# One more wo chunk kept on chip, a 2 KB zero source, and zero writes at other places in a two-layer decode backward

## The chip, the cores and the metric

The kernel runs on one core of one Trainium2 chip. The metric is the device time of the execution in microseconds; the median of five runs is 452.57 us. Engines are named as in the profile: PE (matrix), PEld (its weight loads), DVE (vector), ACT (scalar), POOL (GpSimd) and SP (which here only issues DMAs).

## What is computed

The forward pass of four residual steps on one token of width 1024 (attention, MLP, attention, MLP, with the same weights both times), and its gradients. The output is the token after the four steps, and the gradients of the token, both caches and all weights.

```python
def _A_ref(x, k_cache, v_cache, wq, wo):      # 32 query heads of 128, 4 cache heads
    W = min(4096, max(256, Sk // 4))          # Sk = 32768: the last 4096 rows count
    k, v = k_cache[:, :, Sk - W:, :], v_cache[:, :, Sk - W:, :]   # each repeated for 8 heads
    p = softmax(einsum("bhqd,bhkd->bhqk", (x @ wq) heads, k) * Dh ** -0.5)
    return einsum("bhqk,bhkd->bhqd", p, v) flat @ wo              # wo: 4096 x 1024
def _B_ref(x, w1, b1, w2):                    # F = 3584
    h = x @ w1 + b1
    return (h * tanh(softplus(h))) @ w2
x = x + _A_ref(layernorm(x), ...)   # A1
x = x + _B_ref(layernorm(x), ...)   # B2
x = x + _A_ref(layernorm(x), ...)   # A3
x = x + _B_ref(layernorm(x), ...)   # B4
# reference: x, and vjp of x with respect to A_x, both caches, wq, wo, w1, b1, w2
```

Two consequences matter here. The gradient of each cache is zero outside the last 4096 rows, yet the whole output has to be written: 2 x 4 heads x 28672 rows x 128 in bf16 are 58.7 MB of zeros. And each weight is needed more than once, while the on-chip memory can't hold all of them.

## The kernel before

**Stages.** The order is A1 forward, B2 forward (with the backward products of w2 that B4's gradient needs), A3 forward, "the turn" B4 (`mlp_turn`: forward and backward through w1 block by block), A3 backward, the second pass over w2 (`W2Pass.rest`, which finishes B4's output and gives B2's gradient), B2's w1 pass (`mlp_bwd_w1`), A1 backward, and a last part (L1207 on) that forms all weight and cache gradients as outer products and writes them. Engines run a hand-written order: each issues its instructions in the program's order and waits on what it needs.

**Data on chip.** K, V and wq stay on chip. wo has 16 chunks of 256 rows (512 KB each); chunks 0 to NR - 1 stay in `wo_b`, with NR = 9. The other chunks of wo ("late"), w1 and w2 are streamed through the pool `strm`, which has NB = 6 slots of 4 KB per partition. A load into a slot can be issued when the last reader of the slot is done; SP issues all loads in program order, so a load that waits for a slot holds up whatever stands behind it.

**wo's late chunks.** There are 7 of them for 6 slots in A3 forward (L465 to L467 and L555), A3 backward and A1 backward (L798, and `T` at L807). So six are asked for ahead, and the seventh when a slot comes free. In `attn_fwd` the first 13 (second layer) chunks go through wide matmuls into one row bank and the last 3 through small ones (`fwd_rows2`); `order` (L541) takes one late chunk, then the kept ones, then the other late ones. In `attn_bwd` each late chunk costs one block of eight PE transposes with an ACT copy, and one DVE multiply-and-sum at L813; kept chunks 0 to 7 go through 32 wide matmuls (L833), and the kept chunk 8 through `bwd_rows2` (16 small ones), from weights that `fill` transposed before, in B4. After its loads, A1 backward calls `zeros(Z["A1d"])` (L860).

**Zeros.** 112 jobs of 512 KB each write from one on-chip tile of zeros `zt`, 128 partitions of 4 KB. `bg_zeros(n, after)` (L133) issues n of them on POOL, behind a one-column copy (`gate_t`) that waits until `after` is written; `zeros(n)` (L127) issues n on SP. The table `Z` (L1133) says how many at each place: 76 on POOL in all, in the order B2 (at the w2 loop's last chunk but one), A3 (after q), the seven blocks of B4, A3 backward at its beginning (A3c) and after its loads (A3d), the w1 pass, A1 backward (A1c); the remaining 36 on SP (A1d), ahead of all gradient writes in SP's order.

**Work in gaps.** `fill` takes transposes of wo, V, K and wq (for later stages) from queues, in the order given; `warm(n)` issues n matmuls of 512 columns that nothing reads. Three hooks put w2 work of the second pass into gaps of A3 backward: `copy` (transposes of chunk 0), `sel` (the rest of chunk 0) and `ln` (chunks 1 and 2).

**Constants.** `onesD` is a 128 x 128 fp32 tile of 1/1024, the weights of the matmuls that sum over partitions in the layer norms. `pat` is four copies of a 128 x 32 pattern `fold`; its one 128-column matmul sums each head's column over four groups (L529, L913). `pad_cols` keeps four copies of a 32-column result for `row_layout` to transpose at once.

Of the kernel before, what the change touches and what calls it, by code (L numbers as in the profile page):

```python
# [8 lines left out]
FP32 = mybir.dt.float32  # L9
# [10 lines left out]
NR = 9  # L20
# [3 lines left out]
def kernel(  # L24
# [74 lines left out]
    onesD = keep.tile([P, P], FP32, name="onesD")  # L99
    nc.vector.memset(onesD[:], invD)  # L100
# [15 lines left out]
    zt = keep.tile([P, ZC], BF16, name="zt")  # L116
    nc.gpsimd.memset(zt[:], 0.0)

    zero_jobs = []
    per = ZR // P * DH  # L120
    for out_t in (out_2, out_3):
        for g in range(G):
            zflat = out_t[0, g, 0:ZR, :].rearrange("(p r) d -> p (r d)", p=P)
            for i in range(per // ZC):
                zero_jobs.append(zflat[:, i * ZC:(i + 1) * ZC])

    def zeros(n):  # L127
        for _ in range(min(n, len(zero_jobs))):
            nc.sync.dma_start(zero_jobs.pop(0), zt[:])
# [3 lines left out]
    def bg_zeros(n, after):  # L133
# [3 lines left out]
        for _ in range(min(n, len(zero_jobs))):  # L137
            nc.gpsimd.dma_start(zero_jobs.pop(0), zt[:])  # L138
# [123 lines left out]

    pre = []
# [13 lines left out]
    def ln_fwd(x_col, name):  # L277
# [4 lines left out]
        nc.tensor.matmul(sps[:], lhsT=onesD[:], rhs=xx[:], start=True, stop=True)  # L282
# [17 lines left out]
    def ln_bwd(dn_ps, n32, rstd, g_col, name, nxt):  # L300
# [5 lines left out]
        nc.tensor.matmul(sps[:], lhsT=onesD[:], rhs=tt[:], start=True, stop=True)  # L306
# [83 lines left out]
    def row_layout(col32, name):  # L390
        x = area[name].rearrange("p (g d) -> p g d", g=G)
        ps = psum1([P, P], BF16, "rps")
        nc.tensor.transpose(ps[:, 0:P], col32[:], ident_bf[:])
# [8 lines left out]
    def pad_cols(pad, src_ps, sc, name):  # L402
        nc.scalar.activation(pad[:].rearrange("p (g x) -> p g x", x=40)[:, :, 0:8],
                             src_ps.rearrange("p (g h) -> p g h", g=G), ACT.Copy, scale=sc)
        rep = keep.tile([P, NC, HQ], BF16, name=name + "_rep")
        nc.vector.tensor_copy(
            rep[:].rearrange("p c (g h) -> p c g h", g=G),
            pad[:].rearrange("p (g x) -> p g x", x=40)[:, None, :, 0:8].to_broadcast([P, NC, G, 8]))
# [24 lines left out]
    def attn_fwd(x_col, lname, first):  # L433
# [73 lines left out]
        nc.vector.tensor_scalar(out=sdg[:, 0:32], in0=pat[:, 0, :], scalar1=ssum[:, 0:1], scalar2=None, op0=ALU.mult)  # L507
        sps = sm_tile(P, HQ)
        nc.tensor.matmul(sps[:, 0:32], lhsT=onesD[:], rhs=sdg[:, 0:32], start=True, stop=True)
# [19 lines left out]
        nc.tensor.matmul(lps[:], lhsT=pat[:].rearrange("p c x -> p (c x)"), rhs=ssum[:], start=True, stop=True)  # L529
# [11 lines left out]
        order = early + late if first else late[0:1] + early + late[1:]  # L541
        for i, c in enumerate(order):
# [12 lines left out]
            if not first and i == 0:  # L555
                held[NO - 1] = wo_load(NO - 1)
# [49 lines left out]
    class W2Pass:  # L606
# [33 lines left out]
        def rest(self, done, g_bf, x_col, xname, gbc, zn, last=None):  # L640
            for c in range(NW2):
# [9 lines left out]
                if c == NW2 - 2 and zn:  # L651
                    bg_zeros(zn, self.wg[:, c, :])
# [8 lines left out]
    def mlp_fwd(x_col, lname, g_bf):  # L661
# [5 lines left out]
        gbc = bcast_row(g_bf)  # L667
        for i in range(2 * TD):
            t, hf = i // 2, i % 2
            w = w1_load(i)  # L670
            for b in range(NW2):
# [121 lines left out]
    def attn_bwd(g_col, g_bf, lname, sv, first, nxt):  # L793
# [36 lines left out]
        bwd_rows2(dacc, wo_kept[NR - 1], NR - 1, g_bf, started=False)  # L830
# [7 lines left out]
        if not first:  # L838
# [7 lines left out]
                lambda: row_layout(sA3["dorep"][:].rearrange("p c x -> p (c x)"), "do3"),  # L846
                lambda: row_layout(sA3["qrep"][:].rearrange("p c x -> p (c x)"), "q3"),
# [44 lines left out]
        else:  # L892
# [6 lines left out]
                lambda: row_layout(sA1["dorep"][:].rearrange("p c x -> p (c x)"), "do1"),  # L899
                lambda: row_layout(sA1["qrep"][:].rearrange("p c x -> p (c x)"), "q1"),  # L900
# [11 lines left out]
        for hf in range(2):  # L912
            nc.tensor.matmul(lps[:], lhsT=pat[:].rearrange("p c x -> p (c x)"), rhs=sdp[:, hf:hf + 1], start=hf == 0, stop=hf == 1)  # L913
# [43 lines left out]
    def col_out(cols, n, out_flat):  # L957
        ps = psum1([2 * HQ, P], BF16, "rw")
        nc.tensor.transpose(ps[0:n, 0:P], cols, ident_bf[:])
        rt = work.tile([2 * HQ, P], BF16, name="rt", tag="rt")  # L960
# [172 lines left out]
    Z = dict(B2=3, A3=16, B4=[5, 2, 1, 2, 1, 2, 6], A3c=6, A3d=26, W1=3, A1c=3, A1d=36)  # L1133
# [4 lines left out]
    pat = keep.tile([P, NC, 32], FP32, name="pat")  # L1138
# [6 lines left out]
    fold16f = work.tile([HQ, NO], FP32, name="fold16f")  # L1145

    def constants():
        nc.vector.reduce_sum(fold[:], ident_f[:].rearrange("p (c x) -> p x c", c=NC), axis=AX.X)
        nc.vector.tensor_copy(pat[:], fold[:, None, :].to_broadcast([P, NC, 32]))
# [106 lines left out]
```

## Time and profile before

| | |
|---|---|
| median of 5 runs (451 to 457) | 452.57 us |
| the profiled execution, its own time | 454.31 us |
| its span, first to last instruction | 452.2 us |
| PE, DVE, ACT, POOL busy | 325.1, 236.6, 225.1, 56.8 us |
| DMA | 172.25 MB, mean 381 GB/s |
| queue of SP (q1), of POOL (q0) | 131.61 MB, 39.86 MB |
| zeros | 76 on POOL, 36 on SP, 512 KB each |
| loads of late wo chunks | 28, of 512 KB |

The profiler recorded one execution. "Busy" is time in which an engine had an instruction in work, as a part of the whole span; the stages have different limits, so the shares say little about any one of them. The page's second part cuts the span into 40 equal slices of 11.3 us; a digit is a busy share in tenths, the row of GB/s is what DMA moved in the slice. The stages lie about here: A1 forward to 68 us, B2 to 111, A3 forward to 142, B4 to 188, A3 backward to 246, the second w2 pass to 266, the w1 pass to 295, A1 backward to 338, the gradients to the end. A row of the timeline has the start, the duration, engine, line, operation, output and inputs, shape and count; in brackets stands the idle time of the engine before it and what ended it. "SPq" and "POOLq" are DMAs issued there.

### The profile page before, as it was taken

What the parts mean: (1) busy time and instruction counts of PE and PEld (TensorE: products, weight loads), DVE (VectorE), ACT (ScalarE), POOL (GpSimd) and SP (SyncE); (2) the same over time, 40 slices, a digit from 0 to 9 for tenths busy, and PEclk for the clock granted to TensorE, in tenths of its full rate; (3) what the DMA queues carried; (4) which work ended last, traced back from release to release, by engine and by line L of the source; (5) the groups of instructions that cost most, each with busy time, mean ns of one, the idle gap of its engine ahead of it and who ended that gap; (6) DMA issues with size and microseconds to landing.
All of it is one profiled execution on the core that took longest, in us unless ns stands there. A gap on an engine that the chain in (4) does not pass through costs nothing.

```text
span 452.2 us, 11941 instructions
## 1 busy us (share of the span) xinstructions
PE 325.1 (72%) x5107; PEld 221.0 (49%) x5107; DVE 236.6 (52%) x489; ACT 225.1 (50%) x262; POOL 56.8 (13%) x146
## 2 busy tenths in 40 slices
PE   0565755488997989878899788777877669997400
PEld 0233524387466989855797788744631111121000
DVE  3124101188322757763265954472349889999700
ACT  1122100075242858874484554336219989989600
POOL 2000000001431211432340020042010000000000
PEclk9999555578876989995689678899885555555555
DMA  7999997999999999999998999899999999999994
GB/s 321 381 411 424 408 408 292 409 339 306 416 416 392 397 336 336 398 413 418 414 416 346 328 348 335 310 328 417 416 415 419 419 417 417 419 417 420 417 417 180
DMA packets 52257, 172.25 MB, mean 381 GB/s; under 512 B 5200, under 2 KB 12396, under 8 KB 51180
## 3 DMA queue, kind: packets, MB, share of 16 engines
q1 hardware_dynamic: 41120, 131.61, 75.1%
q0 software_dynamic: 11040, 39.86, 22.1%
q8 instruction: 40, 0.66, 0.6%
q14 instruction: 13, 0.11, 0.1%
q10 hardware_dynamic: 44, 0.01, 0.0%
HBM read 72.89 MB, written 98.58 MB: 379 GB/s over the span
## 4 chain that ended last, share of the span: by engine, by line
PE 19%; DMA 12%; ACT 12%; issue 5%; DVE 3%; POOL 1%; DVEq 0%; SPq 0%; ACTq 0%; POOLq 0%
PE tps L193 7%; ACT wq_b L148 5%; DMA w_c<-in_B_w_dram 4%; PE ops L229 4%; PE acc L229 3%; DMA out_dram<-wo_b 3%; DMA out_dram<-st_o 2%; DMA wo_c<-in_A_wo_dram 2%; ACT wo_b L148 2%; ACT st_o L148 1%; PE d L229 1%; ACT wo_c L148 1%; PE tps L623 1%; ACT K L148 1%; PE sm L229 1%
## 5 line engine op out<-in xcount | busy, mean ns | idle before, releaser
L138 POOL DMA_DIRECT2D out_dram<-zt x76 | 40.6, 537 | 45.1 <-DMA out_dram<-zt 42.5
L229 PEld LDWEIGHTS <-w_c 128*128 128x128 bf16 x1120 | 36.0, 101 | 18.4 <-DMA w_c<-in_B_w_dram 14.2
L229 PE MATMUL ops<-V 2*128 2x512 bf16 (+1 forms) x160 | 34.8, 598 | 5.9 <-ACT wq_b L148 3.3
L633 ACT COPY w_c<-tps 128x1024 bf16<-128x1024 bf16 x28 | 28.2, 1012 | 20.7 <-PE tps L623 11.4
L647 DVE CUSTOM_DVE_ANT_0 scr<-w_c,gbc 128x1024 bf16<-128x1024 bf16 x28 | 34.2, 1221 | 3.7 <-DMA w_c<-in_B_w_dram 2.1
L145 DVE CAST wq_b<-ops 128x1024 bf16<-128x1024 f32 (+1 forms) x31 | 33.8, 1149 | 3.8 <-PE ops L229 3.3
L148 ACT CAST wq_b<-ops 128x1024 bf16<-128x1024 f32 (+1 forms) x33 | 33.7, 1140 | 2.2 <-PE ops L229 2.0
L148 ACT COPY K<-tps 128x1024 bf16<-128x1024 bf16 x19 | 18.7, 1030 | 29.5 <-PE tps L193 29.5
L229 PE MATMUL ops<-wo_b 2*128 2x512 bf16 x120 | 23.3, 568 | 10.9 <-ACT wq_b L148 7.1
L229 PEld LDWEIGHTS <-V 128*128 128x128 bf16 (+2 forms) x416 | 14.1, 101 | 27.8 <-issue 27.6
L229 PE MATMUL q<-wq_b,nA_pair 128*32 128x512 bf16 x128 | 11.9, 454 | 16.3 <-DMA wq_b<-in_A_wq_dram 16.3
L623 PE MATMUL tps<-ident_bf,w_c 128*128 128x128 bf16 x224 | 22.2, 259 | 0.6 <-DMA w_c<-in_B_w_dram 0.6
L148 ACT COPY w_b<-tps 128x1024 bf16<-128x1024 bf16 x20 | 19.5, 1015 | 5.9 <-PE tps L193 5.8
L193 PE MATMUL tps<-ident_bf,w_c 128*128 128x128 bf16 x224 | 19.0, 252 | 4.6 <-DMA w_c<-in_B_w_dram 4.6
L145 DVE COPY K<-tps 128x1024 bf16<-128x1024 bf16 x13 | 8.8, 689 | 24.8 <-PE tps L193 23.0
L193 PE MATMUL tps<-ident_bf,K 128*128 128x128 bf16 x256 | 20.4, 240 | 0.2 <-ACT K L148 0.2
L148 ACT COPY w_c<-tps 128x768 bf16<-128x768 bf16 (+1 forms) x14 | 11.6, 829 | 17.5 <-PE tps L193 17.2
L813 DVE CUSTOM_DVE_ANT_0 wo_c<-wo_c,gbc 128x1024 bf16<-128x1024 bf16 x14 | 16.4, 1218 | 7.3 <-DMA wo_c<-in_A_wo_dram 5.7
L229 PEld LDWEIGHTS <-wo_b 2*128 2x128 bf16 (+1 forms) x152 | 5.6, 99 | 29.3 <-issue 28.6
L145 DVE COPY w_c<-tps 128x1024 bf16<-128x1024 bf16 (+1 forms) x18 | 11.7, 661 | 14.9 <-PE tps L193 10.2
L193 PE MATMUL tps<-ident_bf,wq_b 128*128 128x128 bf16 x256 | 18.4, 241 | 0.9 <-issue 0.9
L193 PEld LDWEIGHTS <-K 128*128 128x128 bf16 x256 | 17.1, 108 | 3.8 <-issue 3.2
(323 smaller groups left out, 664.6 us busy)
## 6 DMA issues: line engine op xcount, KB each, us to landing
out_dram<-zt POOLq DMA_DIRECT2D x76, 512.0 KB, 10.5
out_dram<-zt SPq DMA_DIRECT2D x36, 512.0 KB, 8.7
wo_c<-in_A_wo_dram SPq DMA_DIRECT2D x28, 512.0 KB, 8.4
w_c<-in_B_w_dram SPq DMA_DIRECT2D x32, 448.0 KB, 6.4
w_c<-in_B_w_dram SPq DMA_DIRECT2D x28, 512.0 KB, 6.4
out_dram<-wq_b SPq DMA_DIRECT2D x17, 512.0 KB, 11.5
wq_b<-in_A_wq_dram SPq DMA_DIRECT2D x16, 512.0 KB, 11.2
out_dram<-K SPq DMA_DIRECT2D x8, 1024.0 KB, 12.8
```

What stands on the lines that cost most here:

```text
L138: nc.gpsimd.dma_start(zero_jobs.pop(0), zt[:])
L145: nc.vector.tensor_copy(out_ap, in_ap)
L148: nc.scalar.copy(out_ap, in_ap)
L193: nc.tensor.transpose(ps[:, b, :], ap, ident_bf[:])
L229: nc.tensor.matmul(out_ap, lhsT=lhsT, rhs=rhs, start=start, stop=stop, skip_group_check=True, **kw)
L623: nc.tensor.transpose(self.ps[c][:, b, :], w[:, 1, b * P:(b + 1) * P], ident_bf[:])
L633: nc.scalar.copy(self.w[c][:, 1, :], self.ps.pop(c)[:].rearrange("p b c -> p (b c)"))
L647: nc.vector.tensor_tensor_reduce(out=scr[:], in0=w[:, 0, :], in1=gbc[:], scale=1.0, scalar=0.0, op0=ALU.mult, op1=ALU.add, accum_out=self. ...
L813: nc.vector.tensor_tensor_reduce(out=w[:, 0, :], in0=w[:, 0, :], in1=gbc[:], scale=1.0, scalar=0.0, op0=ALU.mult, op1=ALU.add, accum_out=w ...
```

## The change

- NR is 10: chunk 9 of wo stays on chip as well, and 6 late chunks are streamed, so all six are asked for ahead and the late seventh load is gone (L555 and its like). `order` in the second forward attention takes three late chunks first. `attn_bwd` runs `bwd_rows2` for chunks 8 and 9.
- The memory for it comes from smaller constants: `zt` has 2 KB per partition, and each zero job reads it twice (a broadcast dimension of 2 in the source); `onesD` is one column, read as a broadcast; `pat` is gone, and `over_groups` issues four 32-column matmuls with `fold`; `pad_cols` keeps one copy, and `row_layout` issues four 32-column matmuls into an fp32 bank; two small tiles share buffers with others.
- Zeros: two at B2's w1 loop (new, B2a), two at the first w2 chunk of B2 (new) and three at the last but one as before, 17 for 16 in A3, B4's blocks 1, 2, 2, 2, 2, 2, 3 for 5, 2, 1, 2, 1, 2, 6, A3d 24 for 26, two at chunk 2 of the second w2 pass (new), 4 for 3 at the w1 pass. That is 77 on POOL and 35 on SP.
- In B2 the row copy `gbc` is made after four chunks of w1 instead of ahead of the first.
- The hooks issue 3, 2 and 4 warm matmuls more, and `ln` takes chunk 1 alone; chunk 2 goes back to the second pass.

```diff
-NR = 9
+NR = 10
...
-    onesD = keep.tile([P, P], FP32, name="onesD")
-    nc.vector.memset(onesD[:], invD)
+    ones1 = keep.tile([P, 1], FP32, name="ones1")
+    nc.vector.memset(ones1[:], invD)
+    onesD = ones1[:, 0:1].to_broadcast([P, P])
...
-    zt = keep.tile([P, ZC], BF16, name="zt")
+    zt = keep.tile([P, ZC // 2], BF16, name="zt")
     nc.gpsimd.memset(zt[:], 0.0)
+    zt2 = zt[:, None, :].to_broadcast([P, 2, ZC // 2])
...
-                zero_jobs.append(zflat[:, i * ZC:(i + 1) * ZC])
+                zero_jobs.append(zflat[:, i * ZC:(i + 1) * ZC].rearrange("p (a b) -> p a b", a=2))
...
-            nc.sync.dma_start(zero_jobs.pop(0), zt[:])
+            nc.sync.dma_start(zero_jobs.pop(0), zt2)
...
-            nc.gpsimd.dma_start(zero_jobs.pop(0), zt[:])
+            nc.gpsimd.dma_start(zero_jobs.pop(0), zt2)
...
+    def over_groups(out, rhs, start, stop):
+        for c in range(NC):
+            mm(out[32 * c:32 * c + 32, :], fold[:], rhs, start, stop, tile_position=(0, 32 * c))
...
-        ps = psum1([P, P], BF16, "rps")
-        nc.tensor.transpose(ps[:, 0:P], col32[:], ident_bf[:])
+        ps = psum1([P, P], FP32, "rps")
+        for c in range(NC):
+            mm(ps[32 * c:32 * c + 32, 0:P], col32[:], ident_bf[:], True, True, tile_position=(0, 32 * c))
...
-        nc.tensor.matmul(lps[:], lhsT=pat[:].rearrange("p c x -> p (c x)"), rhs=ssum[:], start=True, stop=True)
+        over_groups(lps, ssum[:], True, True)
...
-        order = early + late if first else late[0:1] + early + late[1:]
+        order = early + late if first else late[0:3] + early + late[3:]
...
-            if not first and i == 0:
-                held[NO - 1] = wo_load(NO - 1)
...
-                if c == NW2 - 2 and zn:
-                    bg_zeros(zn, self.wg[:, c, :])
+                if c in zn:
+                    bg_zeros(zn[c], self.wg[:, c, :])
...
-        gbc = bcast_row(g_bf)
         for i in range(2 * TD):
             t, hf = i // 2, i % 2
             w = w1_load(i)
+            if i == 4:
+                gbc = bcast_row(g_bf)
+                bg_zeros(Z["B2a"], n_bf)
...
-        bwd_rows2(dacc, wo_kept[NR - 1], NR - 1, g_bf, started=False)
+        for c in range(8, NR):
+            bwd_rows2(dacc, wo_kept[c], c, g_bf, started=c > 8)
...
-    Z = dict(B2=3, A3=16, B4=[5, 2, 1, 2, 1, 2, 6], A3c=6, A3d=26, W1=3, A1c=3, A1d=36)
+    Z = dict(B2a=2, B2={0: 2, NW2 - 2: 3}, A3=17, B4=[1, 2, 2, 2, 2, 2, 3], A3c=6, A3d=24, B4w={2: 2}, W1=4, A1c=3, A1d=37)
...
-    hooks.update(copy=lambda: w2p.tp(0), sel=lambda: w2_ahead([0]), ln=lambda: w2_ahead([1, 2]))
+    def copy_gap():
+        w2p.tp(0)
+        warm(3)
+
+    def sel_gap():
+        w2_ahead([0])
+        warm(2)
+
+    def ln_gap():
+        w2_ahead([1])
+        warm(4)
+
+    hooks.update(copy=copy_gap, sel=sel_gap, ln=ln_gap)
     g2, g2b = attn_bwd(g3, g3b, "A3", sA3, True, "B2")
-    x4, wg2 = w2p.rest(3, g2b, x3, "x_B4", bcast_row(g2b), 0)
+    x4, wg2 = w2p.rest(2, g2b, x3, "x_B4", bcast_row(g2b), Z["B4w"])
```

## The prediction

> **What bounds the kernel now.** I read the page's 40 slices first, then the busy times by stage, the timeline around each idle stretch, and the DMA queues by window. All times below are inside the profiled execution: span 452.2 us, its own time 454.31 us, so 2.1 us lie around the span; the median of the runs is 452.57 us.
>
> ```profile
> span 452.2 us, 11941 instructions
> ...
> PEclk9999555578876989995689678899885555555555
> DMA  7999997999999999999998999899999999999994
> GB/s 321 381 411 424 408 408 292 409 339 306 416 416 392 397 336 336 398 413 418 414 416 346 328 348 335 310 328 417 416 415 419 419 417 417 419 417 420 417 417 180
> ```
>
> DMA is busy everywhere, but only some slices move what the queues can, about 417 GB/s. From slice 27 (305 us) to the end every slice is there: the tail is a plain queue of writes. In slices 21 to 26 only 310 to 348 GB/s move: something else sets the pace.
>
> ```profile
> core 0: us, PE busy (x) PEld busy (x) DVE busy (x) ACT busy (x) POOL busy (x), PEclk, DMA share, GB/s
> ...
> 187.00:246.00 59.00, 50.50 (x873) 42.17 (x871) 28.46 (x62) 37.24 (x42) 17.58 (x34) 0.83 1.02 413
> 246.00:266.00 20.00, 15.83 (x374) 14.97 (x370) 17.53 (x31) 11.34 (x12) 0.00 (x0) 0.74 0.88 306
> ...
> 295.00:305.00 10.00, 7.45 (x117) 4.92 (x118) 8.53 (x18) 3.45 (x4) 5.12 (x13) 1.00 0.95 331
> 305.00:446.00 141.00, 95.40 (x784) 30.21 (x780) 93.85 (x119) 94.61 (x100) 6.19 (x35) 0.59 1.02 416
> ```
>
> So time = (when the tail starts) + (bytes left)/416 GB/s + 6 us of ending. Before the tail a chain of dependent stages (PE, then DVE or ACT, then PE) sets the time and waits for a load here and there. A zero written before the tail shortens it; a zero written where a load is awaited lengthens the chain. The waits that the change touches:
>
> ```profile
> 101.80 1.22 DVE L647 CUSTOM_DVE_ANT_0 scr<-w_c,gbc 128x1024 bf16<-128x1024 bf16 x1 [1.48 <-DMA w_c<-in_B_w_dram]
> ...
> 139.71 0.59 PE L229 MATMUL sm<-o_pair,wo_c 128*128 128x16 bf16 x16 [2.07 <-DMA wo_c<-in_A_wo_dram]
> ...
> 160.28 0.60 PE L229 MATMUL sm<-nB_pair,w_b 128*128 128x16 bf16 x16 [2.70 <-DMA w_b<-in_B_w_dram]
> ...
> 203.80 1.22 DVE L813 CUSTOM_DVE_ANT_0 wo_c<-wo_c,gbc 128x1024 bf16<-128x1024 bf16 x1 [2.47 <-DMA wo_c<-in_A_wo_dram]
> ```
>
> [...]And SP's own queue at the last backward attention:
>
> ```profile
> 284.98 15.51 SPq L348 DMA_DIRECT2D wo_c<-in_A_wo_dram  x7
> 300.54 6.06 SPq L129 DMA_DIRECT2D out_dram<-zt  x5
> ```
>
> The seventh wo load waits for a streaming slot, and every zero stands behind it in SP's order: the tail begins at 300.54, although the w1 pass ended at 294.7.
>
> **The price of a packet.** Zeros become two pieces of 2 KB in place of one of 4 KB (source row 2 KB, read twice). No 2 KB packet is in this trace. Windows with nearly one size each bound it:
>
> ```profile
> DMA packets 1704, 6.23 MB, mean 415 GB/s; under 512 B 189, under 2 KB 189, under 8 KB 1702
> ...
> q0 software_dynamic: 1702, 6.20, 101.8%
> ...
> DMA packets 1309, 4.18 MB, mean 418 GB/s; under 512 B 144, under 2 KB 144, under 8 KB 1309
> ...
> q1 hardware_dynamic: 1309, 4.18, 103.1%
> ...
> q0 software_dynamic: 451, 1.62, 80.0%
> q1 hardware_dynamic: 411, 0.41, 23.3%
> ```
>
> First (225 to 240 us, zeros alone): 1702 less 189 tiny ones = 1513 packets of 4 KB in 101.8% of 16 x 15 us = 244 us: 161 ns. Second (370 to 380 us, 3.5 KB rows): 165 us / 1165 = 142 ns. So 38 ns per KB and 9 ns for each packet; w_b's 1 KB packets (142 to 149 us: 2323 in 115 us) take 50 ns against 47 from this line. A 2 KB packet is then 85 ns, two are 170: a zero of 0.524 MB rises from 1.26 us to 1.33, +0.07 (5.6%). [...]0 and 0.10 are the ends (0.10 if the 50 ns of 1 KB sets the line).
>
> The last two lines (155 to 160 us) show how the queues share: nearly as many POOL packets as SP packets, so bytes go by packet size, 1.62 against 0.41 MB. Smaller zero packets therefore leave a contending load a larger part: w_b 1 in 3 bytes in place of 1 in 5, wo and w2 2 in 3 in place of 1 in 2.
>
> **The change, part by part** (minus is faster).
>
> 1. B2's w1 loop. The row copy gbc moves behind four chunks. PE's first chunk was held till 72.14; n_bf is there at 70.5, so the first slot comes free 1.7 us sooner and SP's next w1 load with it. DMA was nearly empty from 71 to 74.5. Two zeros (2.66 us) start at about 72: 0.7 us in the hole, the other 1.9 in the way of w1 loads which the loop awaits one by one. Sum +0.2.
> 2. Two zeros at the first w2 chunk of B2 (91.9 us). The loop is DVE's: 14 x 1.26 us, with a wait of 1.48 already. The two delay loads by up to 2.7; six slots give some cover: between 0 and +2.7, I take +1.3.
> 3. Forward attention A3. Six streamed chunks in six slots: the seventh load and its wait of 2.07 go. Three late chunks now come first, so w1 slots free from 132 us rather than 136. The granted clock fell to 0.50 from 139.8 to 146.6, right behind that wait; the V transposes took 4.51 us for 48, against 1.95 for 32 at full clock in the next stage, so 1.6 more. [...]the row shows ACT with three copies of 1.0 in 144.1 to 148.2, which caps it: -0.8. Sum -2.9.
> 4. The turn B4. The 160.28 wait is the sixth w_b chunk, asked for at 142.9 and landed 17 us later among 5 + 2 + 1 zeros that outweighed it 4 to 1. Now it is asked for about 5 us sooner, with 1 + 2 + 2 zeros of half the packet size: -2.7, and -0.8 as the clock stays up (16 transposes took 1.87 there, 1.05 elsewhere). But the middle blocks get 2 zeros each: 2.66 + 2 w_b loads of 1.47 = 5.6 us of DMA for a block of about 5 us. Loads have 8 us from issue to use: 0 to +2, I take +0.5. Sum -3.0.
> 5. Backward attention A3. The seventh chunk is issued at 195.15 and lands at 203.64. Without it DVE has 6 rows of 1.22, and PE/ACT end at about 202.8 by five steps of some 1.1 to 1.3 us from 197.3, against 205.8: -3.0. Chunk 9 as a kept one adds 16 matmuls, 0.55 us, half hidden: +0.3. Its two transposes enter B4's fill and push two K transposes here: six ACT copies (0.94 each) in place of four ahead of dsT. PE's first half (1.75 us of matmuls) covers most: +0.7. Sum -2.0. Zeros left here (33 not 38, one load less) end before PE's chain, so DMA is not next: 6 x 1.26 less, 33 x 0.07 more.
> 6. Warm matmuls in three gaps, one w2 chunk moved out of the last. Nine of 0.21 us at full clock, partly in idle PE time (0.30 before the row selection, 0.14 before the next): +0.6 (0 to +1.5).
> 7. Two zeros at chunk 2 of the second w2 pass: DVE waits only 0.34 there now and chunks land 0.3 to 1.9 us ahead of use: 0 to +2.6, I take +1.0.
> 8. A fourth zero at the w1 pass: 1.3 more bytes' time, but loads get a larger part: 0.
> 9. Tail. One wo load and one SP zero fewer (35, not 36): -2 x 1.26 = -2.5. 38 zeros behind 294.7 (35 on SP, 3 on POOL) x 0.07: +2.7. SP reaches its zeros 5.8 us sooner; 295 to 305 us moved 331 of 416 GB/s, a hole of 2.0 us, of which I fill 1.5. Sum -1.3. Zeros last to about 350 on the old clock, the first gradient write is ready at 344, so no new hole.
> 10. At nothing: broadcast weights (row_mm loads such weights in 0.11 us, as whole ones), four 32-column matmuls for one of 128 (eight such fp32 records in 0.24 us at L488 against 0.58 for the two at L529, and 16 for 4 at L913), the shorter zt memset, the missing pat copy (both in the first 7 us, under the K load), POOL's new gates (nothing but zeros and a pad memset of 0.25 queued behind them), one staging slot more.
>
> Chain: 0.2 + 1.3 - 2.9 - 3.0 - 2.0 + 0.6 + 1.0 = -4.8. With the tail -6.1: span 446.1, own time 448.2, **median 446.5 us** (-1.3%).
>
> **Rivals.**
> - *More than that.* The clock stays up through all stages and the early zeros cost nothing (items 2, 6, 7 at 0, item 3 at 1.6 for the clock, item 4 without +0.5): -6.1 - 4.2 = -10.3, 442 us. For: the clock falls at 160.2 and 139.8 just behind the waits. Against: the DVE loop at 101.80 has no spare time.
> - *Early zeros give it back.* Items 2, 4, 7 at their upper ends (+1.4, +1.5, +1.6): -1.6, 451 us. For: 5.6 us of DMA in a 5 us block. Against: loads' larger part.
> - *Slower: the 2 KB packet is dear.* The tail is pure queue, so its zeros pay in full: 38 x x. The gain of 6.1 is gone when a zero costs 0.16 us more than I say, 0.23 above the old (18%, 95 ns a packet). At 110 ns (37% more, 0.46 us) the tail grows by 38 x 0.39 = 15 more: 461 us. For: no such packet in the trace, and POOL issues twice the pieces (0.53 us a zero now). Against: three sizes on one line.
> - *Nothing happens:* the removed loads were hidden. Excluded by three idle rows above that name them.
>
> **How the numbers follow.** Forecast 0.50, more 0.15, given back 0.22, slower 0.13. A measurement tells 1% here. Faster by over 1% (below 448.0): all of "more" and 0.37 of the forecast's 0.50 = 0.52. Within 1%: the other 0.13 + 0.22 = 0.35. Slower: 0.13. The forecast's own range is 443.5 to 449.5; the range for 8 in 10 runs from 441 (all of "more" but its end) to 456 (given back, with a packet price at 0.10 and more).
>
> **What would show it.** No streamed wo row with a DMA wait in A3, forward or backward; SP's zeros start right behind the sixth wo load, about 5 us plus the chain's shift earlier (near 290); the row at 160.28 without its 2.70; DVE waits at L647 no more than 1.3 us longer in each w2 pass; zero packets of 2 KB at 85 ns and a tail at 395 to 400 GB/s while zeros run. Wrong if packets are 95 ns or more, if L647 waits 3 us or more, or if the last zeros end after the first gradient write is due by far.

## The result, and the profile after

The changed kernel takes 454.96 us (median of 38 runs, 451.6 to 460.36) against 451.65 us (75 runs) before. The ratio is 1.0082, 95% interval 1.0065 to 1.0099: slower by 0.8%, where 1.3% faster was forecast. Executions more than 1.5% above the fastest of their kernel are left out of the ratio, so it is not quite that of the two medians. The page before is of an execution 2.7 us above its median, the page after of one near its median; that is why the two spans (452.2 and 452.6 us) are nearly equal. First the page of the changed kernel, with the rows that were read before:

```profile
span 452.6 us, 12067 instructions
...
PEclk9998565567888699998799768888975555555555
DMA  7999999999999989999997999999999999999998
GB/s 318 388 412 415 407 408 329 412 389 352 394 402 371 342 277 381 377 377 406 415 375 262 344 354 360 313 382 405 394 380 379 404 406 401 402 407 401 407 408 328
...
q1 hardware_dynamic: 45024, 129.52, 75.2%
q0 software_dynamic: 11184, 40.39, 23.3%
```

Slices 27 to 39 (counted from 0) are the tail. Before, they stood at 415 to 420 GB/s, the last one apart. Now the zeros fall to 379, and the gradient writes behind them (from slice 31), whose packets the change doesn't touch, run at 401 to 408. The queues show who was split: SP's q1 went from 41120 packets to 45024 though it moved less, POOL's q0 from 11040 to 11184 for one zero more. 77 zeros of 128 rows are 9856 packets; in halves q0 would hold 9856 more. So POOL still sent 4 KB packets, only SP sent 2 KB ones. The same four stretches as before:

```profile
core 0: us, PE busy (x) PEld busy (x) DVE busy (x) ACT busy (x) POOL busy (x), PEclk, DMA share, GB/s
187.00:246.00 59.00, 51.70 (x950) 43.33 (x947) 29.69 (x72) 39.66 (x45) 22.25 (x32) 0.91 1.00 385
246.00:266.00 20.00, 15.54 (x379) 14.78 (x376) 16.39 (x27) 10.63 (x11) 1.63 (x3) 0.74 0.85 310
295.00:305.00 10.00, 8.98 (x131) 5.57 (x128) 7.25 (x17) 3.49 (x4) 4.23 (x5) 0.83 1.01 382
305.00:446.00 141.00, 96.16 (x796) 31.80 (x796) 95.21 (x119) 93.90 (x100) 7.69 (x43) 0.59 1.03 400
```

The hole at 295 to 305 us is nearly filled (382, it was 331), and then 141 us run at 400 in place of 416. Now the rows of the timeline that answer to the four waits (L647 is L651 now, L229 is L231, L813 is L819):

```profile
102.58 1.22 DVE L651 CUSTOM_DVE_ANT_0 scr<-w_c,gbc 128x1024 bf16<-128x1024 bf16 x1 [1.51 <-DMA w_c<-in_B_w_dram]
...
140.14 1.36 PE L231 MATMUL sm<-o_pair,wo_c 128*128 128x16 bf16 x48
...
148.33 0.56 PE L231 MATMUL sm<-nB_pair,w_b 128*128 128x16 bf16 x16 [1.89 <-DMA w_b<-in_B_w_dram]
150.28 0.60 PE L231 MATMUL sm<-nB_pair,w_b 128*128 128x16 bf16 x16 [1.40 <-DMA w_b<-in_B_w_dram]
...
196.55 1.22 DVE L819 CUSTOM_DVE_ANT_0 wo_c<-wo_c,gbc 128x1024 bf16<-128x1024 bf16 x1 [0.81 <-issue]
...
259.26 1.22 DVE L651 CUSTOM_DVE_ANT_0 scr<-w_c,gbc 128x1024 bf16<-128x1024 bf16 x1 [1.87 <-DMA w_c<-in_B_w_dram]
```

No streamed wo row waits for its DMA any more: 2.07 and 2.47 are gone. In B4 the wait of 2.70 is gone at 160 us, but 1.89 + 1.40 stand at 148 and 150. Before, PE reached the first half-block of w1 only at this time, and didn't wait:

```profile
147.42 0.72 PE L229 MATMUL sm<-nB_pair,w_b 128*128 128x16 bf16 x23
```

The second w2 pass has a wait of 1.87 (0.34 before). And SP's queue:

```profile
289.73 6.26 SPq L354 DMA_DIRECT2D wo_c<-in_A_wo_dram  x6
296.03 7.46 SPq L131 DMA_DIRECT2D out_dram<-zt  x6
```

The zeros start right behind the sixth wo load, as forecast, at 296 though and not near 290.

### The profile page after: what moved, and what is told of

Read it like the earlier page. It is cut to its first block, busy times and chain, and to the rows that moved or that the text cites. A ratio compares the mean times of both kernels' runs of the same rounds, so it can differ in the third digit from the quotient of the medians.

```text
span 452.6 us, 12067 instructions
## 1 busy us (share of the span) xinstructions
PE 326.7 (72%) x5180; PEld 221.3 (49%) x5180; DVE 234.2 (52%) x484; ACT 225.4 (50%) x262; POOL 72.5 (16%) x150
## 3 DMA queue, kind: packets, MB, share of 16 engines
q1 hardware_dynamic: 45024, 129.52, 75.2%
q0 software_dynamic: 11184, 40.39, 23.3%
## 4 chain that ended last, share of the span: by engine, by line
PE 21%; ACT 14%; DMA 7%; issue 4%; SPq 4%; DVE 2%; DVEq 0%; POOL 0%; ACTq 0%; POOLq 0%
PE ops L231 7%; PE tps L195 6%; ACT wq_b L150 5%; DMA w_c<-in_B_w_dram 4%; SPq L131 4%; PE acc L231 4%; ACT K L150 3%; DMA wo_c<-in_A_wo_dram 2%; ACT wo_b L150 2%; ACT st_o L150 2%; DMA out_dram<-zt 2%; ACT V L150 1%; PE tps L627 1%; ACT w_c L637 1%; PE sm L231 1%
## 5 line engine op out<-in xcount | busy, mean ns | idle before, releaser
L140 POOL DMA_DIRECT2D out_dram<-zt x77 | 56.2, 731 | 32.5 <-DMA out_dram<-zt 26.9
L231 PEld LDWEIGHTS <-w_c 128*128 128x128 bf16 x1120 | 36.6, 101 | 23.5 <-DMA w_c<-in_B_w_dram 18.0
L637 ACT COPY w_c<-tps 128x1024 bf16<-128x1024 bf16 x28 | 28.3, 1012 | 24.1 <-PE tps L627 15.7
L231 PE MATMUL ops<-V 2*128 2x512 bf16 (+1 forms) x160 | 34.6, 598 | 5.9 <-ACT wq_b L150 2.8
L651 DVE CUSTOM_DVE_ANT_0 scr<-w_c,gbc 128x1024 bf16<-128x1024 bf16 x28 | 34.2, 1221 | 7.1 <-DMA w_c<-in_B_w_dram 5.6
L147 DVE CAST wq_b<-ops 128x1024 bf16<-128x1024 f32 (+1 forms) x29 | 31.7, 1152 | 3.6 <-PE ops L231 3.1
L150 ACT CAST wq_b<-ops 128x1024 bf16<-128x1024 f32 (+1 forms) x31 | 31.7, 1138 | 2.2 <-PE ops L231 2.0
L231 PE MATMUL ops<-wo_b 2*128 2x512 bf16 x120 | 23.3, 567 | 10.9 <-ACT wq_b L150 6.6
L231 PEld LDWEIGHTS <-V 128*128 128x128 bf16 (+2 forms) x416 | 14.1, 101 | 27.8 <-issue 27.6
L231 PE MATMUL q<-wq_b,nA_pair 128*32 128x512 bf16 x128 | 12.2, 472 | 15.7 <-DMA wq_b<-in_A_wq_dram 15.7
L150 ACT COPY w_b<-tps 128x1024 bf16<-128x1024 bf16 x20 | 19.5, 1015 | 6.1 <-PE tps L195 6.0
L231 PEld LDWEIGHTS <-wo_b 2*128 2x128 bf16 (+1 forms) x184 | 6.4, 98 | 29.3 <-issue 28.6
L231 PE MATMUL acc<-a_pair,w_c 128*128 128x16 bf16 x448 | 15.7, 172 | 6.0 <-DMA w_c<-in_B_w_dram 6.0
L195 PE MATMUL tps<-ident_bf,K 128*128 128x128 bf16 x256 | 18.9, 232 | 0.0
L150 ACT CAST K<-ops 128x1024 bf16<-128x1024 f32 x18 | 17.7, 1014 | 2.5 <-PE ops L231 1.7
L195 PEld LDWEIGHTS <-K 128*128 128x128 bf16 x256 | 16.1, 104 | 4.2 <-issue 4.1
```

What stands on the lines that cost most here:

```text
L140: nc.gpsimd.dma_start(zero_jobs.pop(0), zt2)
L147: nc.vector.tensor_copy(out_ap, in_ap)
L150: nc.scalar.copy(out_ap, in_ap)
L195: nc.tensor.transpose(ps[:, b, :], ap, ident_bf[:])
L231: nc.tensor.matmul(out_ap, lhsT=lhsT, rhs=rhs, start=start, stop=stop, skip_group_check=True, **kw)
L637: nc.scalar.copy(self.w[c][:, 1, :], self.ps.pop(c)[:].rearrange("p b c -> p (b c)"))
```

## The experiments

Ratios are to the kernel before on the same chip, with 95% intervals; 1% is 4.5 us. Where a difference of two ratios is turned into us, it is that share of 451.7. Each expectation sets a theory A against a theory B; what stands behind it says which of them the run supports.

### The parts of the change alone

**e1_zt2**: the kernel before with the 2 KB zero source (`zt`, `zt2` and both `dma_start` lines of the diff, nothing else).

> The kernel before with one edit: the zero tile is 2 KB per partition and each zero write reads it twice. Nothing else changes. Theory A (the SP zeros' packets really are 2 KB and cost more in the tail): 36 SP zeros at about 380 GB/s (1.38 us) instead of 416 (1.26 us) are 36 x 0.12 = +4.3 us, ratio 1.008 to 1.010; POOL zeros keep 4 KB packets, so the stages before the tail keep their times. Theory B (the lower rate of the changed kernel's tail belongs to the run and not to the packets): +0 to +1 us, ratio 1.000 to 1.002.

1.0055 (1.0029 to 1.0080). Between the two theories: SP's zeros cost more, but the gradient writes behind them kept their 418 GB/s. So the 401 to 408 in the changed kernel's tail are not the 2 KB packets as such.

**e2_place**: the kernel before with the new `Z` table, the moved `gbc` and `Z["B4w"]`.

> The kernel before with one edit: the zeros at the changed kernel's places (two in the w1 loop of B2 with the moved row copy, two at the first w2 chunk, B4 as 1 2 2 2 2 2 3, two at chunk 2 of the second w2 pass, A3d 24, four at the w1 pass), all from the 4 KB source. Theory A (zeros among awaited loads cost the chain what they move): +2.5 in B2, +1 to +3 in B4, +2 in the second w2 pass, less 1.3 for the zero fewer in the tail: +3 to +6 us, ratio 1.007 to 1.013. Theory B (the new places are idle spots and the loss comes from elsewhere): -1 to -3 us, ratio 0.994 to 0.998.

1.0130 (1.0079 to 1.0181), six runs. Theory A: with nine chunks the new places cost 5.9 us, 3.6 to 8.2 by the interval.

**e3_oldz**: the changed kernel with the old places, of the zeros and of the row copy `gbc`.

```
-    Z = dict(B2a=2, B2={0: 2, NW2 - 2: 3}, A3=17, B4=[1, 2, 2, 2, 2, 2, 3], A3c=6, A3d=24, B4w={2: 2}, W1=4, ...)
+    Z = dict(B2a=0, B2={NW2 - 2: 3}, A3=16, B4=[5, 2, 1, 2, 1, 2, 6], A3c=6, A3d=26, B4w={}, W1=3, ...)
```

> The changed kernel with the old places of the zeros and the old place of the row copy; ten kept chunks, 2 KB source and warm matmuls stay. Theory A: the kept chunk gives -2 in each A3 attention and fills a hole of about 2 ahead of the tail, the 2 KB packets take +4 back, warm matmuls +0.6: -1 to -2 us, ratio 0.996 to 1.000. Theory B (the tenth chunk and its small matmuls are what costs): still slower, ratio 1.006 to 1.010.

1.0052 (1.0029 to 1.0075): neither. Without the new places the tenth chunk and the 2 KB source together still lose, as much as the source alone. What the chunk gave was lost again somewhere. And in the changed kernel the new places cost only 0.3% (1.0082 - 1.0052, give or take 0.3), not the 1.3% of e2.

**e5_plain10**: the same without `warm(3)`, `warm(2)`, `warm(4)`, and `w2_ahead([1, 2])` again.

> As the changed kernel with the old places of the zeros and the row copy, and without the nine warm matmuls, with chunks 1 and 2 in the last hook again. Ten kept chunks and the 2 KB source alone. Theory A: 0.5 to 1 us below the same kernel with warm matmuls, -2 to -3 us, ratio 0.994 to 0.998. Theory B (the warm matmuls keep the clock up and are needed): 1 to 2 us above it.

1.0036 (1.0009 to 1.0063), which overlaps with e3: what the nine warm matmuls do is below what these runs tell.

### Where the tail's rate went

In the profiles so far, the gradient writes in the tail (400 to 410 us) run at 417 to 418 GB/s in kernels with nine chunks and at 400 to 407 in those with ten. The first idea was the place of the tiles within 64 bytes.

**e6_after_al** and **e7_plain10_al**: the changed kernel and e5 with 32 bytes of padding ahead of the constants; **e8b_zt2_mis**: e1 with the same padding.

```
+    skew = keep.tile([P, 16], BF16, name="skew")
+    nc.gpsimd.memset(skew[:], 0.0)
```

> The changed kernel with an unused tile of 32 bytes per partition ahead of its constants, which moves every later tile by 32 bytes: the zero tile, K and V lie on multiples of 64 bytes again, as in the kernel before, and the streaming and wq tiles 32 off, as before. In the three profiled kernels with ten chunks, 4 KB write packets in the tail take 163 to 166 ns and from about 320 us on 2 KB ones 87 to 88, in the three with nine chunks 159 and 84. Theory A (the addresses do it): 84 and 159 ns in the whole tail, some 130 us at 3% less, -3 to -4 us against the changed kernel, ratio to before 0.999 to 1.002. Theory B (something else of the ten-chunk schedule does it): 88 and 164 ns stay, ratio 1.007 to 1.010.

> Ten kept chunks and the 2 KB source with the old zero places and no warm matmuls, and the same 32 bytes of padding. Theory A: 159 ns in the tail and -3 to -4 us against the same kernel without padding (1.0036), ratio 0.994 to 0.997. Theory B: 1.002 to 1.006 and 164 ns.

> The kernel before with the 2 KB zero source, and the 32 bytes of padding, which here move the zero tile, K and V off the multiples of 64 bytes (the streaming and wq tiles onto them). Theory A: the tail's packets become 87 to 88 and 163 to 166 ns, +3 to +4 us against the same kernel without padding (1.0055), ratio 1.012 to 1.015. Theory B: 84 and 159 ns, ratio 1.004 to 1.007.

1.0127 (1.0078 to 1.0175), 1.0068 (1.0039 to 1.0096) and 1.0103 (1.0044 to 1.0163). Multiples of 64 bytes heal nothing (e7's zeros: 382 GB/s at 325 to 340 us), so that theory fell. But e8b, nine chunks and only shifted, now has a lower rate too: 381 GB/s in that window against 404 in e1. So it isn't the tenth chunk either; some address matters.

**e9_noearly**: the changed kernel with the six early zeros of B2 and the w2 pass moved to A3d (30 for 24), and the row copy at its old place.

> The changed kernel without the six zeros in B2 and the second w2 pass (and the row copy in its old place); the six go to the backward attention A3 (30 there in place of 24). B4 and the w1 pass keep the new counts. Theory A (those six cost the chain about what they move, since the tail gets no fewer): -2 to -4 us against the changed kernel, ratio 0.999 to 1.004. Theory B (B4's denser zeros are what costs, or the placement is worth nothing in this kernel): 1.006 to 1.010.

1.0081 (1.0044 to 1.0119), theory B's number: in the changed kernel itself nothing is seen of what the six cost. The interval leaves room for a gain of 1.7 us. Taken up again below, in a kernel without that loss in the tail.

### The tenth chunk without the 2 KB source

In the program built from the kernel before, the ring of POOL's DMA descriptors takes 16384 bytes of each partition. Made shorter, it pays for a 4 KB zero tile.

```
-    nc = _bacc.Bacc("TRN2", target_bir_lowering=False, num_devices=1)
+    nc = _bacc.Bacc("TRN2", target_bir_lowering=False, num_devices=1, dynamic_dma_scratch_size=8192)
```

**f2_before_scr**: the kernel before with this line alone.

> The kernel before with the shorter descriptor ring alone, as a control of the two kernels that use it. If the ring is long enough for 6 zeros at once: 0.999 to 1.002. If POOL is held up in issuing and the loads' share grows: 0.995 to 1.006, and then the two others are read against this one.

0.9998 (0.9975 to 1.0022). The ring may be halved here at no price that shows.

**f1_plain10_4k**: e5 with this line and `zt = keep.tile([P, ZC], ...)` as before.

> Ten kept chunks with the old zero places, the old hooks and the old 4 KB zero tile; the memory comes from the ring of POOL's DMA descriptors, 8 KB per partition in place of 16. So this is the tenth chunk without the 2 KB packets. Theory A (the 2 KB packets cost their 84 ns each and then set the tail adrift to 163 ns for 4 KB as well): 159 ns through the tail, and 1.57 MB less to move, ratio 0.989 to 0.993. Theory B (the ten-chunk kernel itself slows the tail): 163 to 166 ns, ratio 0.998 to 1.003.

0.9891 (0.9851 to 0.9931): the time is theory A's, the tail theory B's. Its 4 KB zeros ran at 415 GB/s, the gradient writes later at 401, so 2 KB packets aren't needed for slow gradient writes. In time the chunk is worth 4.9 us.

**f3_after_4k**: the changed kernel with this line and the 4 KB tile.

> The changed kernel with the 4 KB zero tile, memory from the shorter descriptor ring; new zero places and warm matmuls as changed. Theory A (2 KB price 1.5 to 2 us, drift 3 to 4 us): -4 to -6 us against the changed kernel, ratio 0.995 to 1.000, and the rest to the kernel above is what the new places cost. Theory B (the loss is the places and hooks): 1.005 to 1.009.

0.9967 (0.9938 to 0.9995), theory A: the 2 KB source, with all that comes of it, is about 1.15% of the changed kernel's time, and new places and warm matmuls account for 0.76% (0.9967 - 0.9891).

**g1_zt2_again**: e1 once more.

> The kernel before with the 2 KB zero source once more (first 1.0055), for the packet times of its tail beside those of the ten-chunk kernels on the same chip. Theory A (2 KB packets can set the tail adrift, by chance): 84 to 88 and 159 to 164 ns, either is possible, ratio 1.004 to 1.010. Theory B (nine chunks never drift): 84 and 159 ns, ratio 1.003 to 1.006.

1.0030 (1.0006 to 1.0054), 84 and 159 ns. With e1's 1.0055 the 2 KB source costs 0.43% on average in this layout, 1.9 us.

### The address of the zero tile

In the built programs the zero tile begins on a multiple of 512 bytes in every kernel so far with the full rate in its tail (before, e1, e2, f2, g1), and 32 or 64 bytes past one in every other (after, e3, e5, e6, e7, e8b, e9, f1, f3). The change takes 480 bytes from the place of `onesD` (512 to 32), and all behind it moves: K, V and the weights as well lie 32 bytes further within 512 bytes than before.

**g2_ten**: the kernel before with ten chunks and nothing else, memory from the ring, zero tile on a multiple of 512.

```
-NR = 9
+NR = 10
...
-            if not first and i == 0:
-                held[NO - 1] = wo_load(NO - 1)
...
-        bwd_rows2(dacc, wo_kept[NR - 1], NR - 1, g_bf, started=False)
+        for c in range(8, NR):
+            bwd_rows2(dacc, wo_kept[c], c, g_bf, started=c > 8)
...
+    ... dynamic_dma_scratch_size=12288)
```

> The kernel before with ten kept chunks and nothing else: 4 KB zero tile, old constants, old zero places, old order of chunks; the 4 KB for the chunk come from POOL's descriptor ring (12 KB for 16). The zero tile begins on a multiple of 512 bytes and K, V and the streaming slots lie where they lay before. Theory A (in the kernels whose tail went adrift the zero tile began 32 or 64 bytes past a multiple of 512; that starts the drift): 159 ns in the whole tail, some 3 us better than the ten chunks of the earlier run (0.9891), ratio 0.980 to 0.985. Theory B (ten chunks bring the drift): 163 ns from about 340 us on, ratio 0.987 to 0.992.

0.9922 (0.9895 to 0.9948). The packets are theory A's (159 ns to the end), the time isn't: no better than f1. The last stretches show why, f1 first:

```profile
430.00:435.00 5.00, 0.00 (x0) 0.00 (x0) 0.00 (x0) 0.00 (x0) 0.00 (x0) 0.50 1.02 407
435.00:440.00 5.00, 0.00 (x0) 0.00 (x0) 0.00 (x0) 0.00 (x0) 0.00 (x0) 0.50 1.02 408
440.00:445.00 5.00, 0.00 (x0) 0.00 (x0) 0.00 (x0) 0.00 (x0) 0.00 (x0) 0.50 0.52 208
```

and g2:

```profile
430.00:435.00 5.00, 0.00 (x0) 0.00 (x0) 0.00 (x0) 0.00 (x0) 0.00 (x0) 0.50 1.02 419
435.00:440.00 5.00, 0.00 (x0) 0.00 (x0) 0.00 (x0) 0.00 (x0) 0.00 (x0) 0.50 0.94 385
440.00:445.00 5.00, 0.00 (x0) 0.00 (x0) 0.00 (x0) 0.00 (x0) 0.00 (x0) 0.50 0.13 55
```

The last two columns are DMA share and GB/s. g2 is done with most bytes 3 us sooner, then little moves (share 0.13, 55 GB/s), and the spans end alike, 446.7 and 445.9, from the same start: POOL's gate of A1 backward, called A1's gate from here on, is at 292.2 and 291.9. A rate read in mid-tail isn't yet an end.

**h1_zt64**: e1 with the zero tile moved by 64 bytes, and with it only the small constants in front of it; K, V and the weights keep their places within 512 bytes.

```
+    skew = keep.tile([P, 32], BF16, name="skew")
...
     zt = keep.tile([P, ZC // 2], BF16, name="zt")
+    skew2 = keep.tile([P, 224], BF16, name="skew2")
```

> The kernel before with the 2 KB zero source, and the zero tile moved by 64 bytes alone (64 bytes of padding before, 448 behind), so that K, V, wq, wo and the streaming slots keep their place within 512 bytes. Theory A: some 25 us after SP's zeros begin the packets go from 84 to 88 ns, and the gradient writes that follow take 163 in place of 159: +3 us against the same kernel without padding (1.0055 and 1.0030), ratio 1.009 to 1.013. Theory B: 84 and 159 ns, ratio 1.002 to 1.006.

1.0089 (1.0054 to 1.0124) against 1.0055 and 1.0030: 0.47% over their mean, give or take 0.4, on the edge of theory A's range.

**h2_after_512**: the changed kernel with 480 bytes of padding in front of its constants. The zero tile is back on a multiple of 512, and K, V and the weights too are where they were within 512 bytes.

```
+    skew = keep.tile([P, 240], BF16, name="skew")
...
+    ... dynamic_dma_scratch_size=15872)
```

> The changed kernel with 480 bytes of padding ahead of its constants (from the descriptor ring, 512 bytes shorter), so that the 2 KB zero tile begins on a multiple of 512 bytes; K, V and the weights lie within 512 bytes as in the kernel before. Theory A: 84 and 159 ns in the tail, -3 to -4 us against the changed kernel, ratio 0.999 to 1.002. Theory B: 88 and 163 ns, ratio 1.006 to 1.010.

0.9999 (0.9969 to 1.0030), theory A: 480 bytes of padding give back 0.83% (give or take 0.35), 3.7 us, all that the changed kernel had lost. How much of it is the zero tile's and how much that of the other tiles, h2 can't tell; only h1 moves the zero tile without them. The same 15 us (325 to 340) of zeros and 10 us (400 to 410) of gradient writes, in the changed kernel:

```profile
325.00:340.00 15.00, 9.81 (x173) 5.14 (x170) 3.33 (x12) 1.80 (x4) 1.17 (x5) 0.77 1.04 380
400.00:410.00 10.00, 9.13 (x58) 2.10 (x56) 10.00 (x10) 9.12 (x10) 0.00 (x0) 0.50 1.02 406
```

in h2:

```profile
325.00:340.00 15.00, 10.21 (x112) 4.98 (x105) 5.21 (x21) 2.97 (x4) 1.71 (x6) 0.73 1.05 406
400.00:410.00 10.00, 9.83 (x68) 2.17 (x62) 9.98 (x9) 8.53 (x10) 0.00 (x0) 0.50 1.03 417
```

in e1, and in h1:

```profile
325.00:340.00 15.00, 10.60 (x180) 6.28 (x178) 5.81 (x22) 3.52 (x5) 1.71 (x6) 0.84 1.05 404
400.00:410.00 10.00, 9.53 (x64) 1.97 (x58) 9.90 (x9) 9.07 (x10) 0.00 (x0) 0.50 1.03 418
```

```profile
325.00:340.00 15.00, 10.94 (x151) 5.94 (x148) 5.23 (x21) 2.94 (x4) 1.71 (x6) 0.76 1.03 384
400.00:410.00 10.00, 9.72 (x64) 1.97 (x60) 9.88 (x10) 8.71 (x9) 0.00 (x0) 0.50 1.03 412
```

Read the last column: 404 to 406 with the tile on a multiple of 512, 380 to 384 without, and the gradient writes behind, from other tiles, lose as well. DMA share is full in all (1.02 to 1.05): the engines aren't idle, each packet takes longer (in the changed kernel 2 KB ones up to 87 to 88 ns for 84, 4 KB ones 163 for 159). The end shows less of it than the rates. From A1's gate to the last instruction the changed kernel takes 155.2 us and h2 153.4, h1 157.5, e1 and g1 156.6 and 156.1: 1.8 and 1.2 us. In h2 the full DMA share ends at about 443 us, 5 us before the span; in the changed kernel at about 450, 2 us before it. The other 2.5 us between these two executions (452.6 and 448.2) arise before A1's gate, almost all in B4 (48.9 against 46.3 us); whether the address does that too or it is scatter isn't shown.

**g3_eleven**: as g2 with `NR = 11` and a ring of 8 KB.

> As the first of these four with eleven kept chunks (the ring at 8 KB), so five late chunks and again 1.57 MB less to move. If the tail is a plain queue and the chain gives a little as well, -3 to -4 us more: ratio 0.972 to 0.978 with a tail at 159 ns. If the chain ahead of the tail sets the time once the sixth and seventh load are gone: 0.980 to 0.985, as with ten.

0.9833 (0.9783 to 0.9883): one more chunk is worth 0.9% more (give or take 0.6), about the 3.8 us that 1.57 MB take at 416 GB/s. By its number it is in the expectation's second range, but the step from g2 is that of the first, and it comes in the tail: 152.1 us from A1's gate to the end against 154.5, with the gate at 292.8 and 292.2. It beats both kernels by keeping more on chip at the old places and the old zero tile.

### Which of the new places cost

Both from g2 (0.9922), same 4 KB zeros, same addresses.

**k1_b4**:

```
-    B4=[5, 2, 1, 2, 1, 2, 6], ... A3d=26
+    B4=[1, 2, 2, 2, 2, 2, 3], ... A3d=31
```

> Ten kept chunks at the old addresses (0.9922) with one edit: B4's blocks write 1 2 2 2 2 2 3 zeros, and the five fewer go to the backward attention (31 for 26). Theory A (B4's new counts are harmless, the early zeros cost): no wait of 2 to 3 us for the sixth half-block of w1, ratio 0.989 to 0.995. Theory B (two zeros in every middle block take more from the loads than the five at the start did, as the changed kernel's trace suggests with +3 us over B4): 0.997 to 1.001.

0.9870 (0.9824 to 0.9916), six runs: theory A. It overlaps with g2, so a gain of B4's counts isn't shown, only that they cost nothing here.

**k2_early**: the six zeros of B2a, B2 chunk 0 and `B4w`, from A3d (20 for 26).

> Ten kept chunks at the old addresses (0.9922) with one edit: two zeros in the w1 loop of B2 (with the moved row copy), two at its first w2 chunk and two at chunk 2 of the second w2 pass, taken from the backward attention's 26 (20 there). Theory A: the six cost the chain what they move (1.26 us each, less what was idle), +2.5 in B2 and +2 in the w2 pass, and the backward attention runs out of zeros before it ends: ratio 1.000 to 1.006. Theory B: they lie in idle spots and B4 carries the cost of the new places: 0.990 to 0.995.

0.9977 (0.9949 to 1.0005): 2.5 us slower than g2 (give or take 1.7), 4.8 than k1. Short of theory A's numbers, but of its sign: here the early zeros cost, B4's counts don't. In the changed kernel e9 had shown no cost of the same six.

What the tenth chunk does in B4 without the new counts shows in g2's timeline,

```profile
144.52 0.56 PE L229 MATMUL sm<-nB_pair,w_b 128*128 128x16 bf16 x16 [0.78 <-DMA w_b<-in_B_w_dram]
155.50 0.56 PE L229 MATMUL sm<-nB_pair,w_b 128*128 128x16 bf16 x16 [1.59 <-DMA w_b<-in_B_w_dram]
160.82 0.59 PE L229 MATMUL sm<-nB_pair,w_b 128*128 128x16 bf16 x16 [4.77 <-DMA w_b<-in_B_w_dram]
```

against k1's:

```profile
166.00 0.56 PE L229 MATMUL sm<-nB_pair,w_b 128*128 128x16 bf16 x16 [0.41 <-DMA w_b<-in_B_w_dram]
```

Seven us of waits against 0.4. The sixth half-block of w1 is asked for at 141.3 us in g2 and at 140.8 in k1, but right behind it POOL issues five zeros in g2 (from 142.2) and two more at 148.3, in k1 one (at 143.1) and two at 149.2. It is the slowest of g2's fourteen, 19.5 us from issue to landing; in k1 none takes more than 10.6. Both from the view of w_b, g2 first:

```profile
DMA to landing us min/median/max: 3.9/9.4/19.5
DMA to landing us min/median/max: 5.0/7.0/10.6
```

## Why the prediction was wrong

Two steps of the forecast failed: item 4, the gain in B4 (-3.0 us forecast, +2.0 in the traces), and item 10, which put the smaller constants at nothing (3.7 us by h2). Item 9 expected too much of the tail besides. The stages, from the starts of POOL's gates in each trace (one execution each):

| us | to A3's start | A3 forward | B4 | A3 backward and w2 pass | w1 pass | A1's gate at |
|---|---|---|---|---|---|---|
| nine chunks, old places (before, f2, e1, g1), mean | 113.9 | 33.0 | 45.1 | 77.4 | 26.8 | 296.2 |
| g2 and f1, old places, mean | 113.7 | 28.3 | 48.6 | 74.7 | 26.7 | 292.0 |
| k1, B4's new counts | 113.4 | 29.3 | 46.2 | 77.2 | 25.9 | 291.9 |
| after, f3, h2, mean | 115.5 | 28.9 | 47.1 | 77.0 | 27.4 | 295.9 |

The other kernels with ten chunks and old places (e3, e5, e7) agree on B4 (51.7, 49.2, 48.0), but have A1's gate at 292.2, 297.1 and 294.1: a single stage of a single trace is good to 2 or 3 us. Point by point, with the items of the forecast:

- **Items 1 and 2, early zeros in B2:** +1.5 forecast, +1.6 in the table. **Items 5 to 7** together -0.4 forecast, -0.4. The sums agree, in part by luck: DVE's first w2 row in B2 comes at 91.5 us for 90.1 (1.4 later, where item 1 had +0.2), and the loop of those rows is 0.6 longer (item 2 had +1.3). k2's +2.5 for all six early zeros is the 2.5 of items 1, 2 and 7.
- **Item 3, A3 forward:** -2.9 forecast, -4.1. The sign was right, the size too small: the wait of 2.07 us is gone, the granted clock from 139.8 to 146.6 us, 0.50 before, is 1.00 now, and V's transposes take 1.95 us for 32, so the whole 1.6 came of which 0.8 was booked. That the wait had lowered the clock was the forecast's estimate and isn't shown: in k1 and h2 PE waits for no wo load in the 3 us ahead of V's transposes, and these take 4.18 and 4.09 us for 48, against 4.51 before.
- **Item 4, B4: here the chain's sum failed.** -3.0 forecast, +2.0 in the table. "Now it is asked for about 5 us sooner" didn't come: in the changed kernel the first five half-blocks were asked for at the old time or later (136.3 to 145.5 against 136.2 to 141.6), and the sixth at 146.4, where it had been 142.9. So the first loads landed no sooner than before, and PE, which was ready for them about 1 us sooner (146.4 against 147.4), waited: 1.89 + 1.40 us at 148 to 150. A3 forward and B4 together gained 2.1 us, not 5.9. And the argument of "half the packet size" fell away on POOL's queue, whose packets stayed 4 KB (q0 above), so a zero's packet still outweighed a 1 KB packet of w_b 4 to 1 (from 140 to 146 us, 480 packets with 1.74 MB on q0 beside 500 with 0.51 MB on q1). B4's new counts did take the long wait away (k1 against g2), but from a base, the ten-chunk kernel, in which B4 had become 3.5 us longer. And what k1 gains in B4 (2.4) it gives back in the next column (2.5), where its five moved zeros are: A1's gate comes at the same time. The rest of B4's extra time is probably chunk 9's two transposes in B4's fill, which item 5 booked elsewhere; that was not tried.
- **Item 8**, a fourth zero at the w1 pass: 0 forecast, +0.6 in the table, within the scatter. It leaned on the same larger part of loads.
- **Chain in all:** -4.8 forecast, -0.3. With item 4 as measured, -4.8 + 5.0 = +0.2.
- **Item 9, tail:** the packet was forecast well: 85 ns, 84 measured, where half of a 4 KB packet's 159 would be 80; and 36 zeros at +0.04 us (404 for 416 GB/s) to +0.07 (the packets' times) make 1.4 to 2.5 us where e1 and g1 give 1.9. h2 takes 0 in all with +1.9 for packets and the chain's -0.3, so the filled hole and the saved transfers are worth about 1.6, not 4.0. Why, stays open; with old constants too, g2 and f1, the tail is only about 1.3 us shorter than before (154.5 and 154.0 against 155.3 and 155.8 in before and f2).
- **Item 10 is the second failing step.** "Broadcast weights ... at nothing" costed the smaller constants by their instructions alone. They also shift every tile behind them, and the zero tile came to lie 32 bytes past a multiple of 512, with K, V and the weights moved too: +3.7 us (after against h2), as much as the whole loss. The 512 bytes that h2 takes from the ring can't be it, since half the ring made no difference (f2).

One more stop stands at a matmul of item 10, and neither the forecast nor a run accounts for it. In A3 forward the sum over the four groups was one matmul in two records before,

```profile
130.76 0.58 PE L529 MATMUL sm<-ssum,pat 128*128 128x1 f32 x2
```

and PE stands idle in the middle of the eight records that replace it:

```profile
133.12 0.27 PE L231 MATMUL sm<-ssum,fold 128*32 128x1 f32 x5
135.52 0.27 PE L231 MATMUL sm<-ssum,fold 128*32 128x1 f32 x3 [2.12 <-issue]
```

The same stop is 1.02 us in f3, 0.81 in h2, 2.11 in f1, and absent in before, f2 and g2, which have the old constants. "issue" means that the profile shows nothing that PE waited for; in the changed kernel a 16 KB load on the instruction queue (q8) is in work from 133.2 to 134.1. k1, with old constants, has such a stop elsewhere (1.55 us at 172.6). So what causes it, and how much of it reaches the time, stays open.

In ratios: tenth chunk -0.78 (g2), early zeros +0.55 (k2), 2 KB packets +0.43 (e1, g1), addresses +0.83 (h2): +1.0%, against +0.82% measured; the rest (B4's counts, the fourth zero, warm matmuls, one SP zero fewer) is within the intervals. Each term is known to some 0.2 to 0.4%, and they need not add: all new places and hooks together cost 0.76 (f3 against f1), the places 0.30 (changed kernel against e3) or 1.30 (e2), the early zeros 0.0 (e9). Of what was undone in the changed kernel itself, the addresses (h2) and the 2 KB source (f3) gave the loss back, the places (e3) a part that its interval barely shows, the early zeros (e9) nothing.

Of the rivals, "early zeros give it back" named the right stages for about a third of the losses in this sum, "the 2 KB packet is dear" the right place for the rest, but at 84 to 88 ns, not 95, and mostly for a reason that it didn't have.

What the address does to a packet was measured, not explained. In the changed kernel, whose zero tile starts 32 bytes past a multiple of 512, SP's 2 KB packets take 84 ns as well for the first 25 us of its zeros, then 87 to 88, and 4 KB gradient writes from other tiles go from 159 to 163; while wq's tiles, 32 bytes off in the kernel before, were written at 159, and f1's and f3's 4 KB zeros, 32 bytes off, at 160. So that the zero tile's start matters with 2 KB packets is shown by h1 (384 GB/s from 325 to 340 us, where e1 has 404). At what step of the address it starts (only 0, 32 and 64 past 512 were run), by what cause, how the slowness outlasts the zeros, and what slows the gradient writes of f1 and f3 (401 and 402 GB/s), whose zeros ran at the full rate, stay open: there K, V and the weights are moved by 32 bytes too. So it is open whether h1's smaller loss, 0.5%, is the zero tile's share of h2's 0.8% or the same within the intervals.

## What to carry to other kernels

A tile that is made smaller moves all tiles behind it (here by 480 bytes, and 480 bytes of padding gave 3.7 us back): compare the addresses of the DMA sources before and after, not only the instructions. A gain in one stage is real only if the next stage's loads land sooner too; else the next stage waits for them (of 5.9 us forecast for A3 forward and B4, 2.1 came). And before on-chip memory is squeezed out of constants, look for a pool that is too large: the descriptor ring gave 8 KB at no price that shows, and eleven kept chunks with it are 1.7% faster.

## What the runs showed of the hardware that was not expected

- POOL turned a source of two 2 KB pieces into 4 KB packets (11184 on q0, with 77 zeros, for 11040 with 76), SP didn't (8960 packets of 2 KB for its 35); but each issue on POOL took longer, 731 ns for 537, as the groups of the kernel before and after show:

```profile
L138 POOL DMA_DIRECT2D out_dram<-zt x76 | 40.6, 537 | 45.1 <-DMA out_dram<-zt 42.5
```

```profile
L140 POOL DMA_DIRECT2D out_dram<-zt x77 | 56.2, 731 | 32.5 <-DMA out_dram<-zt 26.9
```

- From 325 to 340 us, with the queue full, 2 KB packets from a tile on a multiple of 512 bytes run at 404 to 406 GB/s (e1, h2), from one 32 or 64 bytes off at 380 to 384 (after, e7, e8b, h1); 4 KB packets at 415 to 418, on the multiple (g2) and 32 bytes off (f1, f3).
- Halving POOL's descriptor ring from 16 KB to 8 changed nothing (0.9998, 0.9975 to 1.0022), where POOL issues six zeros at once and then one at a time, as earlier ones land.
